# An attention stage with its products with v in one run per head pair, and its sums moved behind the next scores

## The chip, the cores and the metric

The kernel runs on one core of one Trainium2 chip. The metric is the time of one execution on the device in microseconds (us): 1064.72 us is the median of the three runs before (1062.84 to 1065.97). The engines are named as in the profile: PE is TensorE (matrix products and transposes), PEld its weight loads, DVE is VectorE, ACT is ScalarE, POOL is GpSimd, SP is SyncE, which here only issues DMAs. An engine works through its instructions in the order in which they were written into its queue.

## The reference

The kernel computes an attention of 4 batches x 12 heads over 448 positions with head size 64, with soft-capped scores, and two feed-forward layers on its output:

```
scores = q @ k.T / 8;  scores = cap * tanh(scores / cap)
attn   = exp(scores - max) / (sum(exp(scores - max)) + 1e-9)
x      = (attn @ v)  as 1792 x 768
h1     = x @ w_in1;  x1 = (h1 - tanh(h1)) @ w_out1
h2     = x1 @ w_in2; out = (h2 * sigmoid(1.702 * h2)) @ w_out2
```

The weights come as float64, and the kernel converts them on the way. All products are in fp32.

## The kernel before

The first 200 us are attention, the rest the two layers. Only attention is touched by the change, and all of its instructions are pinned: each engine gets them in the order of the code (`pin`). The DMAs on SP are not pinned; the scheduler places them by its own estimate of when they can go.

**Iterations.** Attention has 24 iterations `g`, each one pair of heads. Scores are computed transposed, keys on the partitions, so that their exponentials can be multiplied with v at once. 448 keys make three chunks of 128 and a rest of 64. The rests of two neighbouring iterations (an even one and the odd one behind it) are put together in one tile of 128 partitions, `tl`. An even iteration and the odd one behind it are called a pair of iterations here.

**What one iteration runs, and on what.**
- `scores` (L526): one chunk, two matmuls, one per head, each on 64 of the 128 rows of PE, so that both run beside each other. Chunk 0 of the next iteration is computed in this one.
- `tail_scores` (L536): the rests' scores of two iterations, four small products on quarters of PE.
- `pair_act` (L545, L547): tanh and exp on ACT, two chunks at a time.
- `pair_pv` (L568): one chunk times v, into the PSUM bank `ps_pv` of the iteration, of which there are two.
- `tail_pv` (L577): the rests of both iterations of a pair times v, four small products, into both `ps_pv` banks.
- `key_adds` (L556 to L558): DVE adds the three chunks and the rest, for the softmax's sum.
- `sums_of_two` (L582): PE sums these over the partitions for the pair before, into a PSUM tile `ps_r`; `add_sums` (L605, L90 with `w<-ps_r`) adds that up on DVE.
- `prep` (L505 to L515, L90): transposes of q and k of iteration `g + 3` on PE, copied out of PSUM by DVE.
- `pair_out` (L90 with `xs<-ps_pv`, L592): DVE copies the finished output, and SP stores part of it.
- Beside these run conversions of weights (`conv_*`), reciprocals (`batch_recip`, L610, halves in iterations 7, 8, 13, 14, 19 and 20), the DMA of the reciprocals to DRAM (`wrow`, L615) and back as broadcast rows (`wb`, L621), and the scaling of finished outputs by them (L666, from iteration 10 on).

**What couples the engines.** The PSUM tiles of the transposes (`ps_qk`) and of the sums (`ps_r`) come from one pool of two buffers, `ps_s`, in turn: a new tile waits until DVE has read the one before the last. The order in which they are asked for is sums, q, k in an even iteration and q, k in an odd one. The scores have two buffers of two banks each, read by ACT.

**The order before.** In an even iteration PE runs: scores of chunks 1 and 2, chunk 0 with v, sums of the pair before, the transposes, chunk 0 of the next scores, the small products with v, chunks 1 and 2 with v. In an odd one: scores of chunks 1 and 2, the transposes, chunk 0 with v, chunk 0 of the next scores, the rests' scores, chunks 1 and 2 with v.

Of the kernel before, what the change touches and what calls it, by code (L numbers as in the profile page):

```python
# [40 lines left out]
def attention_moe_moe(ctx, tc, q, k, v, cap, w_in1, w_out1, w_in2, w_out2, out):  # L41
    nc = tc.nc
    B, H, S, D = q.shape
# [516 lines left out]
    def ps_pv(g):  # L560
        if g not in r_t:
            r_t[g] = ps_v.tile([P, 512], F32, tag="v", name="ps_pv")
        return r_t[g]

    def pair_pv(g, c):
        for j in range(2):
            a = slice(j * D, (j + 1) * D)
            pin(nc.tensor.matmul(  # L568
                ps_pv(g)[a, :S], rawv[g][:, j, c, :], tt[g, c][:, j], start=(c == 0 and g % 2 == 0), stop=(c == KC - 1)
            ))  # L570

    def tail_pv(g):
        for n in (g, g + 1):
            r = tail_rows(n)
            for j in range(2):
                a = slice(j * D, (j + 1) * D)
                pin(nc.tensor.matmul(ps_pv(n)[a, :S], vt[n % 4][r, a], tail(g)[r, j], start=(n > g), stop=False))  # L577

    def sums_of_two(g):
        ps = sum_t[g] = ps_s.tile([P, 512], F32, tag="s", name="ps_r")  # L580
# [47 lines left out]
    def attention():  # L628
        wb = {}

        def x_of(g):
            return [n for n, at in enumerate(split_at) if at == g]

        def x_part(n):
            b, i = divmod(n, NP)
            n = S if b == 0 else CUT
            return i, n, slice(b * S, b * S + n)

        load_qk(0, nc.scalar)
        nc.sync.dma_start(out=capr, in_=cap.partition_broadcast(P))  # L640
        nc.vector.tensor_scalar(
            out=cpos.bitcast(U32), in0=capr.bitcast(U32), scalar1=0x7FFFFFFF, scalar2=None, op0=ALU.bitwise_and
        )
        nc.vector.reciprocal(out=tsc, in_=cpos)
        nc.vector.tensor_scalar(out=tsc, in0=tsc, scalar1=QK_SCALE, scalar2=None, op0=ALU.mult)
        load_qk(1)
        load_v(0)
        load_qk(2)
        load_v(1)

        def prep(g):
            prep_q(g)
            prep_k(g)

        prep(0)
        scores(0, 0)
        prep(1)
        tail_scores(0)
        for g in range(NG):
            pair_act(g, (0, KC) if g % 2 == 0 else (0,))  # L660
            if g - 2 in conv_at:
                conv_hi(early[conv_at.index(g - 2)])
            for n in x_of(g):
                i, w, a = x_part(n)
                x = xs[n][:, :w]
                pin(nc.vector.tensor_tensor(out=x, in0=x, in1=wb.pop(n)[:, :w], op=ALU.mult))  # L666
                hi_pool(xh[i][:, a], x)
            scores(g, 1)
            scores(g, 2)
            last_exp = pair_act(g, (1, 2))  # L670
            if g + 1 in conv_at:
                conv_exp(early[conv_at.index(g + 1)])
            load_v(g + 2)
            if g % 2 == 0:
                pair_pv(g, 0)
            if g % 2 == 0 and g > 0:
                sums_of_two(g - 2)
                add_sums(g - 2)
            if g in conv_at:
                conv_low(early[conv_at.index(g)])  # L680
            if g - 1 in conv_at:
                conv_or(early[conv_at.index(g - 1)])
            for n in x_of(g):
                i, w, a = x_part(n)
                lo_pool(xl[i][:, a], xs.pop(n)[:, :w], xh[i][:, a])
            if g - 2 in conv_at:
                conv_lo(early[conv_at.index(g - 2)])
            if g >= NP and g % NP < 3:
                b = g // NP - 1
                if g % NP:  # L690
                    batch_recip(b, g % NP - 1)
            for n in {0: (2,), 1: (3, 4)}.get(g, (g + 3,)):
                prep(n)
            if g % 2:
                pair_pv(g, 0)
            for n in {0: (3, 4)}.get(g, (g + 4,)):
                load_qk(n)
            for n in x_of(g + 1):
                wb[n] = wb_p.tile([P, S], F32, tag="wb", name="wb")
                i, w, a = x_part(n)  # L700
                w_rows(wb[n][:, :w], 0, i, a.start, a.stop)
            if g in (1, 3):
                dbl_dma()
            if g == NG - 1:
                prepare(1)
                hold[0] = True
                for _ in range(12):
                    next(moe_0)
            scores(g + 1, 0)
            if g % 2:  # L710
                tail_scores(g + 1)
            key_adds(g)
            if g % 2 == 0:
                tail_pv(g)
            pair_pv(g, 1)
            pair_pv(g, 2)
            pair_out(g)
        for _ in range(5):
            next(moe_0)
        hold[0] = False  # L720
        sums_of_two(NG - 2)
        add_sums(NG - 2)
        for half in range(2):
            rec = batch_recip(B - 1, half)
        marks.extend((last_exp.ins, rec.ins))
# [617 lines left out]
```

## Time and profile before

| | |
|---|---|
| runs before | 1064.72 us median, 1062.84 to 1065.97 |
| profiled execution | 1063.6 us, of which the span is 1061.8 us |
| mean granted clock of PE | 0.998 |
| PE busy | 1048.6 us, 99% of the span |
| DVE busy | 821.6 us, 77% |
| ACT busy | 692.4 us, 65% |
| POOL busy | 55.5 us, 5% |

The span is the time from the first to the last instruction. The page's slices are 26.5 us long; attention takes the first seven and a half of them. A timeline row gives the start, the duration, the engine, line and operation, what it writes from what, shapes (partitions x elements), how many instructions were merged, and in brackets the time that the engine stood before it and for whom. An fp32 matmul of the code is two instructions in the trace.

### The profile page before, as it was taken

How to read it: one execution, taken by the hardware profiler on the slowest of the kernel's cores; microseconds unless marked ns; L12 is line 12 of the kernel's file. 1: busy time of each engine (PE TensorE's matmuls, PEld its weight loads, DVE VectorE, ACT ScalarE, POOL GpSimd, SP SyncE). 2: the span in 40 equal slices, each digit the busy share in tenths (PEclk: the TensorE clock that was granted, in tenths of full speed). 3: DMA queues.
4: the chain of work that ended last, by engine and by line, in shares of the span. 5: the costliest groups of instructions: out<-in, count | busy, mean ns of one | idle time of the engine just before them, and what ended most of it. 6: DMA issues, size and time to landing. Idle time of an engine off the chain costs nothing.

```text
span 1061.8 us, 15395 instructions
## 1 busy us (share of the span) xinstructions
PE 1048.6 (99%) x5483; PEld 855.9 (81%) x5483; DVE 821.6 (77%) x1097; ACT 692.4 (65%) x958; POOL 55.5 (5%) x56
## 2 busy tenths in 40 slices
PE   9999989999999999999999999999999999999998
PEld 3333323599999998888878888877899999999998
DVE  4689988899996525988999998686799873438973
ACT  6898878788863415656785756655755755657663
POOL 0113242400000000000000000000000000000000
PEclk9999999999999999999999999999999999999999
DMA  6767777775578877887864853799654554444443
GB/s 145 183 187 220 196 189 217 237 249 210 204 228 258 296 239 266 279 297 255 275 226 149 273 188 91 265 319 299 223 171 132 180 163 121 134 126 142 146 135 107
DMA packets 153749, 218.17 MB, mean 205 GB/s; under 512 B 58381, under 2 KB 101705, under 8 KB 153673
## 3 DMA queue, kind: packets, MB, share of 16 engines
q1 hardware_dynamic: 152376, 216.58, 64.6%
q8 instruction: 43, 0.70, 0.3%
q10 hardware_dynamic: 1296, 0.61, 0.2%
q14 instruction: 34, 0.27, 0.1%
HBM read 158.86 MB, written 58.28 MB: 205 GB/s over the span
## 4 chain that ended last, share of the span: by engine, by line
PE 83%; DVE 7%; DMA 6%; issue 2%; ACT 1%; SPq 1%; DVEq 0%; ACTq 0%
PE ps_o L1193 19%; PE ps_h L911 18%; PE ps_h L1091 13%; PE ps_y L951 9%; PE ps_y L1004 9%; PE ps_sc L526 5%; PE ps_pv L568 5%; DMA wd<-in_moe_w_out_dram 1%; DMA wd<-in_moe_w_in_dram 1%; PE ps_r L582 1%; PE ps_tl L536 1%; DMA whole<-s 1%; DVE wl L93 1%; PE ps_pv L577 1%; PE ps_qk L514 1%
## 5 line engine op out<-in xcount | busy, mean ns | idle before, releaser
L81 ACT CAST rh<-gr 128x512 fp32r<-128x512 f32 (+1 forms) x179 | 103.7, 584 | 101.3 <-PE ps_o L1193 65.2
L911 PE MATMUL ps_h<-x,wh 128*128 128x384 f32 (+1 forms) x672 | 152.9, 358 | 0.0
L93 DVE TENSOR_TENSOR rl<-gr,rh 128x512 fp32r<-128x512 f32 (+1 forms) x179 | 113.8, 641 | 26.4 <-ACT rh L81 25.8
L1193 PE MATMUL ps_o<-wh,rl 128*128 128x384 f32 x392 | 130.9, 334 | 0.0
L1193 PE MATMUL ps_o<-wh,rh 128*128 128x384 f32 x392 | 130.9, 334 | 0.0
L1193 PE MATMUL ps_o<-wl,rh 128*128 128x384 f32 x392 | 130.9, 334 | 0.0
L911 PEld LDWEIGHTS ps_h<-x,wh 128*128 128x128 f32 x672 | 121.1, 188 | 12.0 <-issue 0.7
L93 DVE TENSOR_TENSOR wl<-whole,wh 128x768 fp32r<-128x768 f32 (+1 forms) x103 | 93.9, 912 | 14.7 <-ACT wh L81 13.3
L1091 PE MATMUL ps_h<-x,wh 128*128 128x384 f32 (+1 forms) x336 | 97.2, 359 | 0.0
L81 ACT CAST wh<-whole 128x768 fp32r<-128x768 f32 (+1 forms) x103 | 82.4, 800 | 22.7 <-PE ps_h L1091 10.0
L911 PE MATMUL ps_h<-x,wl 128*128 128x384 f32 (+1 forms) x384 | 88.1, 363 | 0.0
L545 ACT ACTIVATE t<-ps_sc,tsc 128x896 f32<-128x896 f32 x72 | 69.8, 1006 | 25.4 <-PE ps_sc L526 24.8
L911 PEld LDWEIGHTS ps_h<-x,wl 128*128 128x128 f32 x384 | 69.8, 188 | 9.7 <-issue 1.4
L1193 PEld LDWEIGHTS ps_o<-wh,rh 128*128 128x128 f32 x392 | 73.6, 188 | 0.0
L1193 PEld LDWEIGHTS ps_o<-wl,rh 128*128 128x128 f32 x392 | 73.6, 188 | 0.0
L1193 PEld LDWEIGHTS ps_o<-wh,rl 128*128 128x128 f32 x392 | 73.6, 188 | 0.0
L547 ACT ACTIVATE t<-t,cpos 128x896 f32<-128x896 f32 x72 | 72.4, 1042 | 0.4
L361 DVE TENSOR_TENSOR gr<-gr 128x512 f32<-128x512 f32 (+2 forms) x112 | 69.2, 645 | 0.8 <-DMA gr<-xa 0.5
L526 PE MATMUL ps_sc<-qk 64*128 64x448 f32 x288 | 68.7, 576 | 0.8 <-ACT qk L81 0.6
L1091 PE MATMUL ps_h<-x,wl 128*128 128x512 f32 (+1 forms) x192 | 69.5, 362 | 0.0
L361 DVE TENSOR_TENSOR part<-ps_h,part 128x512 f32<-128x512 f32 (+1 forms) x48 | 29.8, 621 | 50.8 <-PE ps_h L1091 50.7
L219 DVE SCALAR_TENSOR_TENSOR wr<-wr,wd 128x768 uint32<-128x768 uint32 x48 | 46.6, 972 | 27.5 <-ACT wd L211 21.3
(155 smaller groups left out, 2193.2 us busy)
## 6 DMA issues: line engine op xcount, KB each, us to landing
wd<-in_moe_w_in_dram SPq DMA_DIRECT2D x64, 384.0 KB
wd<-in_moe_w_out_dram SPq DMA_DIRECT2D x29, 768.0 KB
whole<-single SPq DMA_DIRECT2D x36, 384.0 KB
whole<-s SPq DMA_DIRECT2D x33, 384.0 KB
wh<-kept SPq DMA_DIRECT2D x25, 384.0 KB
wl<-kept SPq DMA_DIRECT2D x25, 384.0 KB
single<-wr SPq DMA_DIRECT2D x24, 384.0 KB
whole<-t SPq DMA_DIRECT2D x22, 384.0 KB
```

Source lines behind the costliest of these rows:

```text
L81: pin(nc.scalar.copy(out=dst, in_=src))
L93: return pin(nc.vector.tensor_tensor(out=dst, in0=src, in1=hi.bitcast(F32), op=ALU.subtract))
L361: nc.vector.tensor_tensor(out=out, in0=a, in1=b, op=kind)
L526: pin(nc.tensor.matmul(ps[:, j, :S], qk[a, kc], qk[a, :S], start=True, stop=True))
L545: pin(nc.scalar.activation(out=t, in_=ps[:, :, :S], func=AF.Tanh, scale=tsc))
L547: ins = pin(nc.scalar.activation(out=tt[g, c], in_=tt[g, c], func=AF.Exp, scale=cpos))
L568: pin(nc.tensor.matmul(ps_pv(g)[a, :S], rawv[g][:, j, c, :], tt[g, c][:, j], start=(c == 0 and g % 2 == 0), stop=(c == KC - 1)))
L911: pin(nc.tensor.matmul(ps, w[:, kk, :], x[kk][:, a], start=(m == 0), stop=(m == len(seq) - 1)))
L951: nc.tensor.matmul(bank[e][:, :a1 - a0], w[:, kk, c], x[2 * j + kk][:, a0:a1], start=(j == 0 and m == 0), stop=(j == KF // 2 - 1 and m == ...
L1004: nc.tensor.matmul(ps[e], w[:, kk, c], x, start=(name == head and k == 0 and m == 0), stop=(k == KH - 1 and m == 2), skip_group_check=True,)
L1091: nc.tensor.matmul(ps, w, x, start=(name == head and m == 0), stop=(m == len(seq) - 1), skip_group_check=True,)
L1193: nc.tensor.matmul(ps[n], x[:, t], w[:, kk, :], start=(first and k == 0 and m == 0), stop=(k == KH - 1 and m == 2), skip_group_check=True,)
```

## The change

Five things are written in another place; no function is new.

- Chunk 0 with v is no longer computed early: all three chunks of an iteration stand in one run at its end (in the last iteration chunk 0 stays ahead of the first products of the feed-forward layer).
- The small products with v of a pair move from the even iteration, where they stood behind the next scores, to the odd one, behind the rests' scores of the next pair. The accumulation of an even iteration's bank now begins with its chunk 0 and ends with the small products, hence the new `start` and `stop`.
- The sums of the pair before move from ahead of the transposes to behind the next scores.
- Their addition on DVE (`add_sums`) moves behind `key_adds`.
- `pair_out` of both iterations of a pair is at the end of the odd one.

```diff
@@ pair_pv
-  ps_pv(g)[a, :S], rawv[g][:, j, c, :], tt[g, c][:, j], start=(c == 0 and g % 2 == 0), stop=(c == KC - 1)
+  ps_pv(g)[a, :S], rawv[g][:, j, c, :], tt[g, c][:, j], start=(c == 0 and g % 2 == 0), stop=(c == KC - 1 and g % 2 == 1)
@@ tail_pv
-  pin(nc.tensor.matmul(ps_pv(n)[a, :S], vt[n % 4][r, a], tail(g)[r, j], start=(n > g), stop=False))
+  pin(nc.tensor.matmul(ps_pv(n)[a, :S], vt[n % 4][r, a], tail(g)[r, j], start=(n > g), stop=(n == g)))
@@ attention, in the loop over g
             load_v(g + 2)
-            if g % 2 == 0:
-                pair_pv(g, 0)
-            if g % 2 == 0 and g > 0:
-                sums_of_two(g - 2)
-                add_sums(g - 2)
...
             for n in {0: (2,), 1: (3, 4)}.get(g, (g + 3,)):
                 prep(n)
-            if g % 2:
-                pair_pv(g, 0)
...
             if g == NG - 1:
+                tail_pv(g - 1)
+                pair_pv(g, 0)
                 prepare(1)
...
             scores(g + 1, 0)
             if g % 2:
                 tail_scores(g + 1)
+                if g < NG - 1:
+                    tail_pv(g - 1)
+            elif g:
+                sums_of_two(g - 2)
             key_adds(g)
-            if g % 2 == 0:
-                tail_pv(g)
-            pair_pv(g, 1)
-            pair_pv(g, 2)
-            pair_out(g)
+            if g % 2 == 0 and g:
+                add_sums(g - 2)
+            for c in range(1 if g == NG - 1 else 0, KC):
+                pair_pv(g, c)
+            if g % 2:
+                pair_out(g - 1)
+                pair_out(g)
```

Three places show how the rows move. The first is PE, from the end of iteration 2 to the end of iteration 3, before (one row is one or more matmuls of the code; `x4` is how many):

```order
L577 MATMUL ps_pv<-tl,vt_140 64x448 x2
L577 MATMUL ps_pv<-tl,vt_141 64x448 x2
L568 MATMUL ps_pv<-t,rv 64x448 x4
L526 MATMUL ps_sc<-qk 128x448 x4
L505 MATMUL ps_qk<-ident,raw 128x112 x4
L514 MATMUL ps_qk<-ident,raw 128x128 x3
L515 MATMUL ps_qk<-ident,raw 128x64
L568 MATMUL ps_pv<-t,rv 64x448 x2
L526 MATMUL ps_sc<-qk 128x448 x2
L536 MATMUL ps_tl<-qk 64x448 x4
L568 MATMUL ps_pv<-t,rv 64x448 x4
```

And the same place now:

```order
L582 MATMUL ps_r<-ts,sel 32x448 x4
L568 MATMUL ps_pv<-t,rv 64x448 x6
L526 MATMUL ps_sc<-qk 128x448 x4
L505 MATMUL ps_qk<-ident,raw 128x112 x4
L514 MATMUL ps_qk<-ident,raw 128x128 x3
L515 MATMUL ps_qk<-ident,raw 128x64
L526 MATMUL ps_sc<-qk 128x448 x2
L536 MATMUL ps_tl<-qk 64x448 x4
L577 MATMUL ps_pv<-tl,vt_140 64x448 x2
L577 MATMUL ps_pv<-tl,vt_141 64x448 x2
L568 MATMUL ps_pv<-t,rv 64x448 x6
```

The six products with v stand in one run, the small ones (`vt`) directly behind the rests' scores, the sums directly ahead of the even iteration's run with v, and the scores directly behind the transposes.

The second place is DVE, from the last key addition of iteration 13 through iteration 14, which has a reciprocal, before:

```order
L558 TENSOR_TENSOR ts<-ts,t 128x896
L90 COPY xs<-ps_pv 128x448
L666 TENSOR_TENSOR xs<-xs,wb 128x448
L90 COPY w<-ps_r 128x448
L213 TENSOR_SCALAR wd<-wd 128x768
L610 RECIPROCAL w<-w 128x224
L90 COPY qk<-ps_qk 128x448 x2
L556 TENSOR_TENSOR ts<-t 128x896
L557 TENSOR_TENSOR ts<-ts,tl 64x896
L558 TENSOR_TENSOR ts<-ts,t 128x896
L90 COPY xs<-ps_pv 128x448
```

And now:

```order
L558 TENSOR_TENSOR ts<-ts,t 128x896
L90 COPY xs<-ps_pv 128x448 x2
L666 TENSOR_TENSOR xs<-xs,wb 128x448
L213 TENSOR_SCALAR wd<-wd 128x768
L610 RECIPROCAL w<-w 128x224
L90 COPY qk<-ps_qk 128x448 x2
L556 TENSOR_TENSOR ts<-t 128x896
L557 TENSOR_TENSOR ts<-ts,tl 64x896
L558 TENSOR_TENSOR ts<-ts,t 128x896
L90 COPY w<-ps_r 128x448
```

The copy of the sums has gone behind the key additions, and two output copies stand where one was.

The third place is SP's queue of DMAs around the reciprocals of the second batch, before:

```order
L592 DMA xd_93<-xs 128x448
L465 DMA raw<-in_q_dram 112x4x64 x2
L615 DMA wrow_98<-w 3x320 x4
L615 DMA wrow_99<-w 3x128 x4
L489 DMA rv<-in_v_dram 128x2x192
L621 DMA wb<-wrow_98 64x320
L592 DMA xd_94<-xs 128x448
L621 DMA wb<-wrow_98 64x320
L189 DMA wd<-in_moe_w_in_dram 128x3x256 x2
```

And now:

```order
L592 DMA xd_93<-xs 128x448
L615 DMA wrow_98<-w 3x320 x4
L615 DMA wrow_99<-w 3x128 x4
L621 DMA wb<-wrow_98 64x320 x2
L465 DMA raw<-in_q_dram 112x4x64
L489 DMA rv<-in_v_dram 128x2x192
L465 DMA raw<-in_q_dram 112x4x64
L189 DMA wd<-in_moe_w_in_dram 128x3x256 x2
```

The two broadcast rows stand directly behind the store of the reciprocals, and the two loads of q behind them. On ACT and POOL no row of attention moves, and behind attention no row moves on PE, DVE, ACT or POOL.

## Rows read from the trace of the kernel before

**Rows 1.** The page's busy table: busy time, share of the span, instructions.

```profile
PE 1048.6 (99%) x5483; PEld 855.9 (81%) x5483; DVE 821.6 (77%) x1097; ACT 692.4 (65%) x958; POOL 55.5 (5%) x56
```

**Rows 2.** Stretches: length, busy PE, PEld, DVE, ACT, POOL, clock, DMA, GB/s.

```profile
36.00:52.00 16.00, 15.79 (x92) 5.71 (x90) 11.84 (x15) 13.99 (x15) 3.60 (x2) 1.00 0.60 147
100.00:116.00 16.00, 15.79 (x94) 5.80 (x91) 14.86 (x16) 13.63 (x15) 9.88 (x7) 1.00 0.72 207
120.60:136.20 15.60, 15.39 (x91) 5.52 (x89) 15.04 (x18) 13.96 (x16) 4.68 (x5) 1.00 0.68 200
```

**Rows 3.** Timeline of PE, second half of iteration 12 and iteration 13.

```profile
109.88 1.07 PE L526 MATMUL ps_sc<-qk 64*128 64x448 f32 x4
110.88 0.98 PE L577 MATMUL ps_pv<-tl,vt 64*64 64x448 f32 x8
111.79 1.72 PE L568 MATMUL ps_pv<-t,rv 128*64 128x448 f32 x8
113.44 1.77 PE L526 MATMUL ps_sc<-qk 64*128 64x448 f32 x8
...
116.22 0.97 PE L568 MATMUL ps_pv<-t,rv 128*64 128x448 f32 x4
117.12 1.02 PE L526 MATMUL ps_sc<-qk 64*128 64x448 f32 x4
118.07 0.98 PE L536 MATMUL ps_tl<-qk 64*64 64x448 f32 x8
118.98 1.72 PE L568 MATMUL ps_pv<-t,rv 128*64 128x448 f32 x8
120.64 1.77 PE L526 MATMUL ps_sc<-qk 64*128 64x448 f32 x8
```

**Rows 4.** PE's waits, whole span: us in total, times, longest.

```profile
PE ps_qk L514 <- DVE w L605: 3.9, 6, 2.9
...
PE ps_qk L514 <- DVE w L90: 0.9, 4, 0.2
PE ps_y L1004 <- DVE wl L93: 0.7, 1, 0.7
...
PE ps_qk L514 <- DMA raw<-in_k_dram: 0.5, 1, 0.5
```

**Rows 5.** Who waited for the sums of L582: us, times.

```profile
  DVE w L605: 10.4, 6
  DVE w L90: 5.9, 4
```

**Rows 6.** Timeline of DVE in iteration 14.

```profile
124.27 0.62 DVE L90 COPY w<-ps_r 128x448 f32<-128x448 f32 x1 [0.30 <-PE ps_r L582]
124.81 1.41 DVE L213 TENSOR_SCALAR wd<-wd 128x768 uint32<-128x768 uint16 x1
...
127.61 1.08 DVE L90 COPY qk<-ps_qk 128x448 f32<-128x448 f32 x2
```

**Rows 7.** Timeline of DVE at the start of iteration 16.

```profile
142.67 0.49 DVE L666 TENSOR_TENSOR xs<-xs,wb 128x320 f32<-128x320 f32 x1 [2.78 <-DMA wb<-wrow]
```

**Rows 8.** Timeline of PE in iteration 16.

```profile
143.75 0.55 PE L514 MATMUL ps_qk<-ident,raw 128*128 128x128 f32 x3 [2.86 <-DVE w L605]
...
144.23 1.91 PE L526 MATMUL ps_sc<-qk 64*128 64x448 f32 x4
...
147.78 1.72 PE L568 MATMUL ps_pv<-t,rv 128*64 128x448 f32 x8
```

**Rows 9.** The stretch behind that wait, columns as in rows 2.

```profile
144.00:148.00 4.00, 4.00 (x18) 1.11 (x18) 3.97 (x5) 1.77 (x2) 2.64 (x2) 0.57 0.72 196
```

**Rows 10.** Timeline of SP's DMA issues ahead of that wait.

```profile
130.35 2.27 SPq L465 DMA_DIRECT2D raw<-in_q_dram  x2
132.71 2.65 SPq L615 DMA_DIRECT2D wrow<-w  x8
...
137.07 0.49 SPq L621 DMA_DIRECT2D wb<-wrow  x1
```

## The prediction, made before the changed kernel ran

> **What bounds the kernel now.** The first view to read is the page's busy table: TensorE (PE) is busy for 1048.6 us of the span of 1061.8 [rows 1], so whatever shortens PE's row of work shortens the kernel, and nothing else does. The change lies in the attention stage, which is the first 200 us. The table by stretches shows two regimes there [rows 2]: early, VectorE (DVE) has work for 11.84 us of 16; later, when the finished pairs are scaled as well, for 14.86 of 16 and 15.04 of 15.6. In the second regime DVE is nearly a second bound, and that is what makes the case hard. ScalarE (ACT) has 13.63 to 13.99 in the same stretches and is third.
>
> The timeline of PE shows how its time is made [rows 3]. I read it from start to start, since the ends are modelled. Four instructions of one chunk with v cost 0.90 us when they stand alone (116.22 to 117.12), eight in one run cost 1.65 (111.79 to 113.44), so a further chunk in a run costs 0.75 and a run of its own 0.15 more. The small products of the rests' scores cost 0.91 (118.07 to 118.98), those with v also 0.91 (110.88 to 111.79), each as a run of its own. A chunk of scores costs 0.95 ahead of the rests' scores (117.12 to 118.07) and 1.00 straight behind the transposes (109.88 to 110.88).
>
> The table of PE's waits adds the only wait that repeats [rows 4]: the k transposes wait for the addition of the sums out of PSUM, six times for 3.9 us, the longest 2.9, and four short times for 0.9. Without the longest that is 1.9 us in nine pairs, 0.21 each. The counterpart stands on DVE: it idles 10.4 and 5.9 us, 16.3 in ten even iterations, until the sums are there [rows 5].
>
> **The change part by part.** No matmul is added or removed; three things move.
>
> *Chunk 0 joins chunks 1 and 2.* One run of 12 costs 1.65 + 0.75 = 2.40 in place of 0.90 + 1.65: 0.15 less in each iteration. In odd ones the scores now stand behind the transposes, at 1.00 for 0.95: 0.05 back.
>
> *The small products with v move from the even iteration behind the rests' scores of the odd one.* Both are runs of the same shape, so I cost the second at the step of a further chunk, 0.75 for 0.91: 0.16 less. No row shows these two adjacent; the bounds are 0.91 (no gain) and 0.75. I take 0.75, since every run of one shape in the rows continues at that step.
>
> A chunk of scores costs 0.05 more behind the transposes than behind a run with v, although the last transpose and the scores use PE in one shape (64 rows, 128 columns). The Trainium skill ("TensorEngine Tiling (Array Packing)", Key Properties) says that changing the tiling mode drains TensorE. By it a pair's ten changes of shape in place of fourteen would give 4 x 0.15 and the 0.21 of the wait below, 0.81 for the 0.62 that I work out, 1.9 us more over ten pairs. This row speaks against it, so the sum goes by the rows.
>
> *The sums move from ahead of the transposes to behind the next scores, and their addition on DVE behind the key additions.* The 0.21 wait goes. For a pair in the steady state: even 0.15 + 0.21, odd 0.15 - 0.05 + 0.16, together 0.62. Ten even and nine odd iterations with transposes (2 to 20): 10 x 0.36 + 9 x 0.26 = **5.9 us** off PE's row. The last three iterations have no transposes, and there the scores also merge; I give them 0.5, because ACT is close behind PE there.
>
> *The start.* In iteration 1 PE waits 0.47 us for raw k to land [rows 4]. The small products leave iteration 0, ahead of that transfer, and return behind it. An odd iteration grows by 0.75 - 0.15 + 0.05 = **0.65 us**, and here no shorter even one makes up for it.
>
> *A new wait.* The PSUM buffers of transposes and sums are a ring of two. The order was sums, q, k; it is now q, k, sums. So sums must wait until DVE has copied out this iteration's q, where before they waited for a copy of the iteration before. PE asks for that buffer 2.78 us (scores and transposes, 113.44 to 116.22) plus 1.00 into the even iteration, at 3.78. If it is late, the three chunks with v and the next scores queue behind sums, and ACT after them. Iteration 14, which has a reciprocal, is the worst place [rows 6]: the iteration starts at 120.64 and the q and k copies at 127.61, 6.97 later; two copies take 1.08, so q is out at 7.51. Of this the idle 0.30 before the sums' addition goes, the addition (0.54) is replaced by the second output copy (half of 1.08), and the odd iteration before is 0.65 longer: 6.56, that is 2.8 late. One iteration stands in the rows for four of this pattern: the same working gives 1.8 at iteration 8, 1.0 at 12 and 0.4 at 20, and up to 1 for the k transposes of 13, which need the sums' addition; at the others q is out in time. From the other side the cost is nothing: the 16.3 us that DVE gets back lie in the iterations before these [rows 5], and each stall gives DVE time to catch up. Both ends, 0 and 6.9; the DVE rows of the busy stretch are nearer to the late end, the early ones to the other, and I take **3.2**.
>
> *The event at 140 us.* Once DVE waits 2.78 us for the broadcast row `wb` [rows 7]. It holds the sums' addition, PE's k transposes wait 2.86 behind it [rows 8], and in the next 4 us PE is granted 0.57 of its clock, a stretch partly at 1.2 GHz instead of 2.4 [rows 9]. The scores and the small products then take 3.55 (144.23 to 147.78) for 1.91 (109.88 to 111.79). Price: 2.86 + 1.64 = 4.5 us. The change moves the DMAs: `wb` is issued straight behind `wrow`, without two loads of q ahead (2.27) and without a v load and an output between (135.36 to 137.07 less one `wb`, 1.2) [rows 10]. `wb` would be some 3.5 us earlier, at 139.2, while DVE asked at 142.67 - 2.78 = 139.9 and will ask perhaps 1.5 earlier. A wait of about 0.7 remains, and sums now stand later. Ends: 0 and 4.5 of gain; I take **3.3**, as the order of the issues is nearest to the row of the transfer.
>
> Sum: 0.65 - 5.9 - 0.5 - 3.3 + 3.2 = -5.9 us. Behind attention PE has no wait over 0.7 us [rows 4], and its order there is the same, so the gain passes to the end. The profiled execution took 1063.6 us, 1.8 around the span; 1063.6 - 5.9 = 1057.7. The median of the runs shown is 1.1 above that execution: **1058.8 us**.
>
> **Rivals.**
> *DVE takes it all back.* All stalls come (6.9) and the `wb` wait stays: 0.65 - 5.9 - 0.5 + 6.9 = +1.2, 1065.9. For it speaks 15.04 of 15.6 us [rows 2], against it the idle time handed back.
> *Free of stalls.* DVE is always ahead and the event goes: 0.65 - 5.9 - 0.5 - 4.5 = -10.3, 1054.4. For it speak the 11.84 us of the early regime, against it the reciprocals.
> *Sums stand behind the reciprocal, and the clock falls.* If DVE uses the returned time for nothing (its three additions wait for ACT's exponentials all the same), q is out at 7.51 in iterations 8, 14 and 20, PE stands 3.7 us each time, and a stand of 2.86 already cost 1.64 in clock: 3 x 5.3 = 16.0, with 1.0 at 12. That gives 0.65 - 5.9 - 0.5 - 3.3 + 17.0 = +8.0, 1072.7. It makes the kernel slower once the stalls together pass 9.1 us. Against it speaks that DVE's time is mostly work, not waits, in front of these copies.
>
> **How the numbers follow.** Forecast 0.50, DVE takes it all 0.20, free of stalls 0.18, clock falls 0.12. About 0.3%, 3.2 us, is what a measurement of this kernel can tell. Of the forecast's half, which runs from 1054.5 to 1062.5, nine tenths lie below 1061.5; with the stall-free case and a little of the first rival: faster 0.62. The rest of these is within: 0.26. Slower 0.12. The range reaches from the stall-free case (1054.4, and 0.9 below it for merged runs that may give more) to the first rival (1065.9): 1053.5 to 1066.
>
> **What would show it.** Runs of 12 with v at 2.4 us and the small products at about 1.66 with the rests' scores; no wait of k transposes for the sums' addition in most pairs; instead waits of sums for the q copies, at 8, 12 and 14 first; the clock at 1.00 from 144 to 148. The steady pair 0.6 shorter in the early regime, less in the later. Wrong would be a small step of 0.91 behind the rests' scores, waits of sums in every even iteration, or a granted clock that falls in other places.

## The result, and the profile after

| | before | changed |
|---|---|---|
| median of five runs | 1065.06 us (1062.84 to 1065.97) | 1055.68 us (1054.08 to 1056.18) |
| ratio, with its 95% interval | | 0.9912 [0.9898, 0.9927] |
| profiled execution, span | 1063.6, 1061.8 | 1055.68, 1053.9 |

The kernel is faster by 9.4 us of the medians; 5.9 were forecast (1058.8, range 1053.5 to 1066). The page's busy table answers to [rows 1]:

```profile
PE 1038.7 (99%) x5483; PEld 857.8 (81%) x5483; DVE 819.6 (78%) x1097; ACT 692.0 (66%) x958; POOL 56.1 (5%) x56
```

The number of PE's instructions is the same, its busy time 9.9 us less, the other engines' within 2 us. The same matmuls stand in fewer separate runs, and PE's granted clock is 1.00 throughout.

Three stretches of attention, with the columns of [rows 2]:

```profile
36.00:52.00 16.00, 16.00 (x100) 6.76 (x100) 12.75 (x18) 15.44 (x18) 2.66 (x2) 1.00 0.66 168
100.00:116.00 16.00, 14.09 (x86) 5.42 (x84) 15.69 (x17) 13.86 (x16) 6.53 (x4) 1.00 0.72 191
116.00:132.00 16.00, 15.29 (x94) 5.99 (x92) 15.19 (x20) 13.17 (x15) 5.98 (x5) 1.00 0.65 191
```

Early, PE has no gap at all and ACT is at 15.44 of 16. Around iteration 13 (the second row) PE has gaps of 1.9 us, and DVE is at 15.69: there DVE sets the time, as experiment 8 shows for this place.

An undisturbed pair of iterations on PE, odd (from its transposes) and even, for [rows 3]:

```profile
51.64 0.27 PE L515 MATMUL ps_qk<-ident,raw 64*128 64x64 f32 x1
51.65 1.07 PE L526 MATMUL ps_sc<-qk 64*128 64x448 f32 x4
52.65 0.98 PE L536 MATMUL ps_tl<-qk 64*64 64x448 f32 x8
53.45 0.93 PE L577 MATMUL ps_pv<-tl,vt 64*64 64x448 f32 x8
54.32 2.48 PE L568 MATMUL ps_pv<-t,rv 128*64 128x448 f32 x12
56.72 1.77 PE L526 MATMUL ps_sc<-qk 64*128 64x448 f32 x8
58.43 0.60 PE L505 MATMUL ps_qk<-ident,raw 112*128 112x112 f32 x4
58.87 0.49 PE L514 MATMUL ps_qk<-ident,raw 128*128 128x128 f32 x3
59.29 0.27 PE L515 MATMUL ps_qk<-ident,raw 64*128 64x64 f32 x1
59.30 1.07 PE L526 MATMUL ps_sc<-qk 64*128 64x448 f32 x4
60.30 0.96 PE L582 MATMUL ps_r<-ts,sel 128*32 128x448 f32 x8
61.19 2.48 PE L568 MATMUL ps_pv<-t,rv 128*64 128x448 f32 x12
```

The run of 12 with v takes 2.40 (54.32 to 56.72), rests' scores and small products together 1.67 (52.65 to 54.32). Both are as forecast. The 64-row transpose (L515) and the scores behind it start 0.01 apart; this is what the forecast did not see (below). PE's waits in attention, for [rows 4] (us in total, times, longest):

```profile
PE ps_r L582 <- DVE qk L90: 2.8, 4, 1.2
PE ps_qk L514 <- DVE w L605: 1.8, 2, 1.2
PE ps_sc L526 <- ACT t L545: 1.5, 3, 0.7
```

The k transposes' wait for the sums' addition is gone from all but two iterations; in its place sums wait for the q copies in 8, 12, 14 and 20 (0.23, 0.67, 0.71 and 1.21), the places of the forecast. The two of the second row are at 13 (1.23) and 19 (0.56). The cause of the one at 13 stands on DVE and POOL; here are the three key additions of iteration 12 and the sums' addition on DVE, then, in the same time, POOL's last step on an output and its part of a weight conversion:

```profile
105.30 1.61 DVE L556 TENSOR_TENSOR ts<-t 128x896 f32<-128x896 f32 x1
106.94 1.59 DVE L557 TENSOR_TENSOR ts<-ts,tl 64x896 f32<-64x896 f32 x1
108.64 2.52 DVE L558 TENSOR_TENSOR ts<-ts,t 128x896 f32<-128x896 f32 x1
111.08 0.61 DVE L605 TENSOR_TENSOR w<-w,ps_r 128x448 f32<-128x448 f32 x1
```

```profile
104.81 1.15 POOL L87 TENSOR_TENSOR x<-xs,x 128x448 fp32r<-128x448 f32 x1
105.90 1.69 POOL L84 CAST wh<-wr 128x768 fp32r<-128x768 f32 x1
107.67 2.53 POOL L87 TENSOR_TENSOR wl<-wr,wh 128x768 fp32r<-128x768 f32 x1
```

Of the 72 additions 51 take 1.08 or 1.09. The third here, queued at 108.64, ends 0.96 behind POOL's subtraction, and the first two end 0.95 and 0.94 behind the POOL operations of 104.81 and 105.90. The Trainium skill ("SBUF — State Buffer", "SBUF: two separate sides") says that a DVE operation with two SBUF inputs and a GpSimd operation that reads SBUF exclude each other for whole instructions; the trace agrees, 2.52 for 1.09.

The event at 140 us is gone. SP issues the reciprocals' rows as follows, for [rows 10], and the stretch of [rows 9] now has the full clock:

```profile
126.38 2.50 SPq L615 DMA_DIRECT2D wrow<-w  x8
128.93 1.12 SPq L621 DMA_DIRECT2D wb<-wrow  x2
...
132.17 1.08 SPq L189 DMA_DIRECT2D wd<-in_moe_w_in_dram  x2
```

```profile
144.00:148.00 4.00, 4.00 (x28) 1.34 (x22) 3.86 (x4) 4.00 (x6) 1.74 (x2) 1.00 0.65 205
```

**Where the time went.** I count from the first of an iteration's eight scores instructions to the next iteration's. A normal even iteration went from 8.36 to 6.87, an odd one from 7.20 to 7.65: a pair from 15.56 to 14.52, 1.04 less. Over ten even (-1.49 each) and nine odd iterations (+0.45 each) that is -10.85. The event was 13.23 - 8.36 = 4.87 and is gone. What iterations take above these normal values in the changed kernel, the stalls, is 5.42 (0.31, 0.75, 1.45, 0.78, 0.07, 0.78, 1.28 at 8, 12, 13, 14, 17, 19, 20). The last three iterations give +0.42, the start -0.04, and a start-up that was 0.43 longer in this execution lies ahead of all that. Together -9.5; the first product behind attention starts at 187.84 for 197.32, -9.48.

Behind attention 1.6 of it are lost in the two profiled executions (span -7.9), but not in the medians (-9.4): the profiled execution of before lay 1.5 under its own median.

### The profile page after: what moved, and what is told of

Read it like the earlier page. It is cut to its first block, busy times and chain, and to the rows that moved or that the text cites. A ratio compares the mean times of both kernels' runs of the same rounds, so it can differ in the third digit from the quotient of the medians.

```text
span 1053.9 us, 15397 instructions
## 1 busy us (share of the span) xinstructions
PE 1038.7 (99%) x5483; PEld 857.8 (81%) x5483; DVE 819.6 (78%) x1097; ACT 692.0 (66%) x958; POOL 56.1 (5%) x56
## 4 chain that ended last, share of the span: by engine, by line
PE 81%; DVE 11%; ACT 3%; DMA 3%; issue 2%; SPq 0%; DVEq 0%; ACTq 0%
PE ps_o L1194 19%; PE ps_h L912 19%; PE ps_h L1092 19%; PE ps_y L952 9%; PE ps_y L1005 5%; PE ps_pv L568 3%; PE ps_sc L526 3%; DVE gr L361 1%; DVE wl L93 1%; ACT t L545 1%; DVE rl L93 1%; DVE ts L557 1%; PE ps_r L582 1%; DVE ts L556 1%; PE ps_tl L536 1%
```

## The experiments

Iteration times below are read from starts of scores in each profile. "2 to 7" is from the start of iteration 2 to that of 8, "8 to 19" from there to the start of 20; "16" is that iteration. The ratio is to runs of the kernel before on the same chip; those had medians of 1064.52 (experiments 1 to 4), 1064.21 (5 to 8), 1065.51 (9 to 11) and 1063.76 (12).

| kernel | 2 to 7 | 8 to 19 | 16 | median us | ratio [95%] |
|---|---|---|---|---|---|
| before | 46.68 | 98.21 | 13.23 | | |
| changed | 43.56 | 91.25 | 6.87 | 1055.68 | 0.9912 [0.9898, 0.9927] |
| 1 run with v merged | 45.33 | 99.31 | 16.20 | 1063.28 | 0.9992 [0.9977, 1.0006] |
| 2 small products moved | 46.19 | 96.32 | 8.51 | 1068.08 | 1.0032 [1.0014, 1.0050] |
| 3 sums moved | 45.38 | 91.77 | 7.94 | 1057.95 | 0.9941 [0.9924, 0.9958] |
| 4 rows issued earlier | 46.68 | 96.87 | 8.99 | 1063.99 | 0.9994 [0.9977, 1.0012] |
| 5 64-row transpose first | 45.32 | 92.38 | 7.17 | 1058.39 | 0.9941 [0.9927, 0.9955] |
| 6 reciprocals late | 43.56 | 96.84 | 14.18 | 1060.30 | 0.9963 [0.9949, 0.9977] |
| 7 sums last | 43.56 | 92.01 | 7.15 | 1056.98 | 0.9926 [0.9913, 0.9940] |
| 8 conversions late | 43.56 | 94.81 | 6.87 | 1074.02 | 1.0084 [1.0066, 1.0101] |
| 9 four reciprocals late | 43.56 | 93.90 | 6.87 | 1057.63 | 0.9929 [0.9913, 0.9945] |
| 10 last step late | 43.56 | 94.14 | 7.35 | 1066.03 | 1.0011 [0.9998, 1.0024] |
| 11 = 9 and 10 | 43.56 | 94.53 | 7.36 | 1067.13 | 1.0014 [1.0001, 1.0028] |
| 12 merged, sums moved | 44.04 | 92.80 | 8.53 | 1058.88 | 0.9952 [0.9934, 0.9970] |

### One part of the change at a time (from the kernel before)

**1. The run with v merged, nothing else.**

```diff
-            if g % 2 == 0:
-                pair_pv(g, 0)
...
-            if g % 2:
+            if g == NG - 1:
                 pair_pv(g, 0)
...
-            pair_pv(g, 1)
-            pair_pv(g, 2)
+            for c in range(1 if g == NG - 1 else 0, KC):
+                pair_pv(g, c)
```

(`start` and `stop` follow the new order here and in experiment 2; those lines are left out.)

> The kernel before, with chunk 0 with v joined to chunks 1 and 2 in one run in every iteration; the sums, their addition and the small products stay where they stood. Theory (every change of the shape in which PE is used costs 0.15 to 0.20 us, from transposes to scores too): 0.15 less in the even and 0.30 to 0.35 less in the odd iterations, about 0.45 to 0.5 per pair, 4.5 to 5 us over ten pairs, so about 1060 against 1065; the scores behind the transposes of an odd iteration start 0.87 after the last transposes' run began. The wait of the k transposes for the sums' addition stays, and so does the event at iteration 16. Rival (the prediction's reading: scores behind transposes cost 0.05 more than scores behind a run with v, nothing is saved there): 0.15 and 0.10, 0.25 per pair, 2.5 us, about 1062.5. Second rival (DVE bounds the stage): nothing at all, DVE's waits shrink by as much.

Even iterations 8.22, odd 6.90: 0.15 and 0.30 less, as the theory has it, against the prediction's 0.15 and 0.10. The median is only 1.2 us lower, which the interval does not tell from nothing: the iterations before and behind are shorter, but the event grew to 16.20 - 8.22 = 8.0 us. The even iteration in this kernel still has the sums ahead of the transposes:

```profile
60.16 0.60 PE L505 MATMUL ps_qk<-ident,raw 112*128 112x112 f32 x4
60.97 0.55 PE L514 MATMUL ps_qk<-ident,raw 128*128 128x128 f32 x3 [0.21 <-DVE w L605]
61.45 0.27 PE L515 MATMUL ps_qk<-ident,raw 64*128 64x64 f32 x1
61.46 1.07 PE L526 MATMUL ps_sc<-qk 64*128 64x448 f32 x4
```

From the q transposes to the scores 1.30, where the changed kernel has 0.87 (58.43 to 59.30): 0.43, of which the trace calls only 0.21 a wait. The rest is in the steps around it: q's run lasts 0.81 for 0.44, which is 0.16 more than the wait, and k's 0.48 for 0.42.

**2. The small products moved, nothing else.**

```diff
             if g % 2:
                 tail_scores(g + 1)
+                tail_pv(g - 1)
             key_adds(g)
-            if g % 2 == 0:
-                tail_pv(g)
...
-            pair_out(g)
+            if g % 2:
+                pair_out(g - 1)
+                pair_out(g)
```

> The kernel before, with the small products with v of a pair moved behind the rests' scores of the odd iteration, and both outputs copied at its end; chunk 0 with v and the sums stay. Theory: the two small runs of one shape side by side save one change of shape, 0.15 to 0.2 per pair (an odd iteration longer by about 0.75, an even one shorter by 0.91 and by the change to chunks 1 and 2), 1.5 to 2 us over ten pairs, about 1063.3. Rival (prediction: 0.16 per pair off, 0.65 lost at the start): about 1064. If the event at iteration 16 goes with it (it hangs on the order of SP), another 4.9 less: then about 1058.5.

Undisturbed iterations take 7.45 and 7.94, a pair 15.39, 0.17 less: the term of 0.16 was right. But the median is 3.6 us worse, which no theory had. Chunk 0 with v stands early in this kernel, and it now meets ACT:

```profile
PE ps_pv L568 <- ACT t L545: 6.2, 6, 2.1
```

The longest of these waits, 2.08 in iteration 22, is followed by a granted clock of 0.57 from 190 to 194, and that iteration takes 9.84 for 8.05. The profiled execution (1065.0) lies 3.1 under its median, so this trace does not show all of the loss.

**3. The sums moved, nothing else.**

```diff
-            if g % 2 == 0 and g > 0:
-                sums_of_two(g - 2)
-                add_sums(g - 2)
...
             if g % 2:
                 tail_scores(g + 1)
+            elif g:
+                sums_of_two(g - 2)
             key_adds(g)
+            if g % 2 == 0 and g:
+                add_sums(g - 2)
```

> The kernel before, with only the sums moved behind the next scores and their addition on DVE behind the key additions. Theory: the k transposes no longer stand behind the sums' addition, which in the timelines cost 0.43 in each even iteration (1.30 from the q run to the k run before, 0.87 after); 0.43 x 10 = 4.3 us less, minus the new waits of sums for the q copies, about 2 to 3 us: about 1063. The wait of 2.86 of iteration 16 moves off the transposes but stays on DVE if the broadcast row is as late. Rival (the prediction's 0.21 per pair out of the table of waits): 2.1 minus 2 to 3, so no change, 1065. The trace tells the two apart without the stalls: the even iteration without a stall is 7.9 by the theory, 8.15 by the rival, from 8.36.

Even iterations 7.94: 0.43 less, the theory's number. The stalls that both theories deducted hardly came (0.79 at 13 and 0.21 at 14, 0.06 at 20), and the event is gone too, its broadcast row being issued at 127.33. This one edit gives 6.6 of the 9.4 us; the event alone is 4.9 in the trace.

The three parts add up where nothing else interferes: in iterations 2 to 7 they take 1.35, 0.49 and 1.30 off 46.68, which makes 43.54; the changed kernel has 43.56. From 8 on they don't: the two that lie on top of the sums would bring another 0.61 per pair, 3.7 in six pairs, and the stretch falls only from 91.77 to 91.25.

**4. The rows of the reciprocals issued earlier; PE, DVE, ACT and POOL as before.**

```diff
+                    with tc.high_priority(offset=120):
                         nc.sync.dma_start(out=wrow[p][n, :, a:z], in_=...)
...
+                if p == 0:
+                    first_of_all.enter_context(tc.high_priority(offset=120))
                 nc.sync.dma_start(out=t[j * D:(j + 1) * D], in_=wrow[p]...)
```

> The kernel before, with the rows of work on PE, DVE, ACT and POOL unchanged; only the DMAs of the reciprocals to DRAM and back are issued earlier on SP. Theory: the event at iteration 16 is the order of SP's queue and nothing else; with the broadcast rows in time it is gone whole, 4.9 us (the iteration takes 8.36 for 13.23): about 1060. Rival (prediction's figure): 3.3 less and a wait of 0.7 left, about 1061.8. Second rival: the transfer is late for the loads it shares the DMA engines with; then nothing, 1065, and DVE still waits more than 2 us for it.

The event is gone (8.99, of which 0.27 a wait for the addition), and DVE waits 0.19 for the row. Yet the median is not clearly lower: three transfers of raw k are now late, and PE waits 0.63 and 1.08 in 17 and 0.86 in 19 for them (17 takes 9.17 and 19 takes 8.12 for 7.20). The place in SP's queue is what the row won and what k lost. The first expectation was right on the event and wrong on the time, since it left out who would lose the place. What decided whether the row was late shows when SP's orders are put side by side: the row's second transfer was issued at 137.07 before (2.78 of wait), 136.07 with the run merged, and in this kernel at 136.75. Before (both halves of the row), with the run merged, then in this kernel:

```profile
135.90 0.50 SPq L621 DMA_DIRECT2D wb<-wrow  x1
...
137.07 0.49 SPq L621 DMA_DIRECT2D wb<-wrow  x1
137.67 1.07 SPq L189 DMA_DIRECT2D wd<-in_moe_w_in_dram  x2
```

```profile
136.07 0.49 SPq L621 DMA_DIRECT2D wb<-wrow  x1
136.67 1.06 SPq L189 DMA_DIRECT2D wd<-in_moe_w_in_dram  x2
```

```profile
136.75 1.77 SPq L625 DMA_DIRECT2D wb<-wrow  x3
138.57 0.58 SPq L592 DMA_DIRECT2D xd<-xs  x1
139.25 1.05 SPq L189 DMA_DIRECT2D wd<-in_moe_w_in_dram  x2
```

And what DVE waited for the row with the run merged:

```profile
141.48 0.49 DVE L666 TENSOR_TENSOR xs<-xs,wb 128x320 f32<-128x320 f32 x1 [5.34 <-DMA wb<-wrow]
```

With a weight load (`wd`) issued 0.6 us behind it, the row arrived 5.4 us after its issue; with the load 2.5 us behind, 2.9. The kernel before has the load 0.60 behind (137.67) and 5.6 to arrival, experiment 6 has it 1.1 ahead and 4.4. These four traces agree, but no run changed the place of the load alone, so this stays a reading. The changed kernel adds nothing to it: its load is 2.7 behind the second half (129.45), but the row is issued 7 us earlier and would be in time either way.

### The price of a change of shape

**5. The 64-row transpose ahead of the three 128-row ones** (from the changed kernel, as all that follow but the last).

```diff
+        pin(nc.tensor.transpose(ps[:, KC * P:S], t[:KT, 1, KC * P:], ident[:KT, :KT]))
...
-        pin(nc.tensor.transpose(ps[:, KC * P:S], t[:KT, 1, KC * P:], ident[:KT, :KT]))
```

> The changed kernel with the 64-row transpose of k ahead of the three 128-row ones, so that a 128-row run stands directly ahead of the scores: the same matmuls, two more changes of shape in each of the 21 iterations with transposes. Theory (a change of shape costs 0.15 to 0.20 us, and scores behind the 64-row transpose pay none): iterations 2 to 7 take 0.3 to 0.4 more each; from 8 on part of it is hidden, since there the stretch from 8 to 20 is set by DVE (91.25 us with the changed kernel, 91.77 with the sums moved alone, though its PE row is 0.6 per pair longer). Sum +3 to +6 us. Rival (the prediction's reading, no price from transposes to scores): no change in iterations 2 to 7 and in the median.

Every iteration from 2 to 7 takes 0.29 or 0.30 more, 1.76 in six: two changes of shape at 0.15 on average. The rival is out.

```profile
52.59 0.27 PE L513 MATMUL ps_qk<-ident,raw 64*128 64x64 f32 x1
52.80 0.55 PE L515 MATMUL ps_qk<-ident,raw 128*128 128x128 f32 x3
53.27 1.02 PE L526 MATMUL ps_sc<-qk 64*128 64x448 f32 x4
```

The small transpose now holds the row for 0.21 instead of 0.01. From 8 to 19 the same twelve additions should cost 3.5, and the stretch grew by 1.1. PE's time is covered there. The median is 2.7 above the changed kernel's, just under the range given; by the ratios it is 3.1.

### What makes the stalls

**6. All reciprocals behind the copies of q and k.**

```diff
+            for n in {0: (2,), 1: (3, 4)}.get(g, (g + 3,)):
+                prep(n)
             if g >= NP and g % NP < 3:
                 b = g // NP - 1
                 if g % NP:
                     batch_recip(b, g % NP - 1)
-            for n in {0: (2,), 1: (3, 4)}.get(g, (g + 3,)):
-                prep(n)
```

> The changed kernel with each half of a reciprocal (1.55 us on DVE, iterations 7, 8, 13, 14, 19, 20) behind the q and k copies of its iteration and not ahead of them. Theory A (the stalls are a matter of order on DVE, a copy behind a reciprocal): the copies are out 1.5 us earlier, the stalls of iterations 8, 13, 14 and 20 (0.31, 1.45, 0.78, 1.28) go: -2.5 to -3.8. Theory B (from iteration 8 on DVE's work sets the time, 85.5 of 91.25 us busy and the rest waits for ACT): the reciprocal then delays the key additions, the sums and the next copies, and the stalls come elsewhere: 0 to -1. A wait of the broadcast rows for the later reciprocal is possible (+0 to +4).

The stalls of 8, 14, 19 and 20 go (6.87, 6.87, 7.65, 6.87), those of 12 and 13 stay. For the four theory A is right: the copies stood behind a reciprocal. But the row of the reciprocals then goes out at 130.23 for 126.38, next to a weight load, DVE waits 5.2 for it, PE stands 5.3 behind that, the clock is at 0.50 from 140 to 144, and iteration 16 takes 7.3 more; I had put that at 4 at most.

**7. The sums at the end of the even iteration.**

```diff
-            elif g:
-                sums_of_two(g - 2)
             key_adds(g)
-            if g % 2 == 0 and g:
-                add_sums(g - 2)
...
+            if g % 2 == 0 and g:
+                sums_of_two(g - 2)
+                add_sums(g - 2)
             if g % 2:
                 pair_out(g - 1)
```

> The changed kernel with the sums and their addition at the end of the even iteration, behind the run with v (2.4 us later on PE, and behind the next iteration's scores on the ring's account). Theory A: sums no longer wait for the q copy (0.67, 0.71, 0.56 and the like at 8, 12, 14, 20: -2 to -2.5), but the transposes of the odd iteration wait for their addition out of the same PSUM ring, 2.8 us behind the sums on PE, DVE having the two output copies of the pair before it no more: together -1 to -2. Theory B (DVE's work sets the time): the stalls only change their place, from sums to transposes, 0 to -0.5 in sum, and the stretch from 8 to 20 stays at about 91 us.

Sums no longer wait, and the transposes of 13 wait longer. The stretch is 92.01, theory B's. (The 0.56 in the expectation was no wait of sums: it is that of the transposes of 19.) Iteration 13 takes 11.36, 3.7 more than normal, and the wait alone (1.97, for 1.23 in the changed kernel) does not explain it; the granted clock behind it does, since 0.38 of 4 us is another 1.5:

```profile
112.00:116.00 4.00, 4.00 (x24) 1.41 (x23) 3.96 (x5) 2.29 (x4) 0.00 (x0) 0.62 0.83 247
```

That is the prediction's third rival, in small. The profiled execution, 1059.33, is the slowest of the six.

**8. The weight conversions beside attention placed later.**

```diff
-    conv_at = [3, 5, 7, 9, 11, 14, 16, 18, 20]
+    conv_at = [3, 5, 7, 9, 15, 17, 18, 20, 21]
```

> The changed kernel with another table of where the weight conversions beside attention stand: 3, 5, 7, 9, 15, 17, 18, 20, 21 for 3, 5, 7, 9, 11, 14, 16, 18, 20. The same work, but DVE has 0.56 + 0.95 less in iterations 11 and 12 and POOL nothing in 13, where the three key additions took 1.61, 1.59 and 2.52 beside POOL's conversions and take 1.09 each without. Theory B (DVE's time sets iterations 12 to 15, 30.9 busy of 32.0 us): the stalls of 13 and 14 go and most of that of 12, 2 to 2.8 us; the conversions added at 15 to 20 lengthen those iterations by up to 1.5; sum -1 to -2.5, and iterations 12 to 15 take 29.5 to 30 for 32.0. Theory A (order on DVE alone): the q copies stay behind additions and reciprocal, stalls of 0.7 stay at 12 and 14, only the 1.2 at 13 shrinks: -0.5 to -1.

Iterations 12 to 15 take 29.04, four normal ones, for 32.02: no stall left, PE without a gap, DVE at 27.56 for 30.89. The columns are those of the stretches above; under it the three additions of iteration 12, one of which still takes 1.71 beside POOL:

```profile
101.41:130.45 29.04, 29.04 (x178) 11.39 (x176) 27.56 (x35) 27.07 (x30) 5.36 (x6) 1.00 0.64 166
```

```profile
105.35 1.71 DVE L556 TENSOR_TENSOR ts<-t 128x896 f32<-128x896 f32 x1
107.09 1.08 DVE L557 TENSOR_TENSOR ts<-ts,tl 64x896 f32<-64x896 f32 x1
108.28 1.09 DVE L558 TENSOR_TENSOR ts<-ts,t 128x896 f32<-128x896 f32 x1
```

Theory B holds for these iterations, reciprocals included, which were not moved here. As a whole it is the worst of all: what was moved stands in the way later (17 takes 11.19 and 19 takes 10.47; PE waits 8.4 us for ACT, for 1.5 in the changed kernel), and the first product behind attention waits 9.6 for a converted weight. I had counted 1.5 for that.

**9. The reciprocals behind the copies only in 7, 8, 19 and 20.**

```diff
+                if g % NP and b == 1:
                     batch_recip(b, g % NP - 1)
...
+            if g >= NP and g % NP in (1, 2) and g // NP != 2:
+                batch_recip(g // NP - 1, g % NP - 1)
```

> The changed kernel with the reciprocal behind the q and k copies in iterations 7, 8, 19 and 20 only; in 13 and 14 it stays ahead, so that the row of the reciprocals goes to DRAM as early as in the changed kernel. Theory (the run with all reciprocals late lost by the broadcast row alone, 7.3 us at iteration 16, and won the stalls of 8, 19 and 20): iteration 16 takes 6.87, 19 and 20 take 7.65 and 6.87 for 8.43 and 8.15; -2 us against the changed kernel, about 1053.5. Rival (the reciprocals' work only moves, DVE's time sets the stretch): iterations 17 to 22 give it back, 0.

Iteration 16 and 20 are as expected (6.87), 8 too. But rows now come late again: DVE waits 5.2 us for them in five places, first 1.35 at iteration 10, and 10, 12 and 17 to 19 take 0.6 to 1.4 more than normal. The gain is given back as the rival has it, but by way of the rows; what part DVE's work has in it stays open.

**10. The last step of a conversion on DVE behind the additions.**

```diff
-            if g - 1 in conv_at:
-                conv_or(early[conv_at.index(g - 1)])
...
             if g % 2 == 0 and g:
                 add_sums(g - 2)
+            if g - 1 in conv_at:
+                conv_or(early[conv_at.index(g - 1)])
```

> The changed kernel with the last step of a weight conversion on DVE (0.95 us, every second even iteration up to 12, then 15, 17, 19, 21) behind the key additions and the sums' addition instead of ahead of the q copy. POOL's part of the conversion is released by it and starts some 5 us later, beside the reciprocal and the copies and not beside the three key additions. Theory (the stall of 1.45 at iteration 13 and those of 0.7 at 12 come from DVE being held by this step and by POOL's part beside its additions): the q copy of 12 is out 0.95 earlier, the additions of 12 take 1.1 to 1.3 each for 1.61, 1.59 and 2.52; stalls of 12 and 13 gone, -2 us, about 1053.5 to 1054. Rival (the additions are slow whatever POOL does, or DVE's work sets the time): the additions still take more than 1.5 each, and no more than 0.75 is gained.

The additions of 12 take 1.81, 1.08 and 1.09, with POOL's part at 111.37, and 13 is normal (7.65): with experiment 8 this shows the conversion as the cause of the stall of 1.45. Its step on DVE and POOL's part moved together, and no run parts them. Iteration 12 keeps its stall (7.76, sums wait 0.82), and 14 takes 8.40 for 7.65: from 12 to 14 only 0.56 is gained (23.81 for 24.37). The stall moved on: at 14 sums wait 1.46 for the q copy, for 0.71 in the changed kernel. Later, conversions on ACT wait 5.4 for their loads, PE waits 5.8 for ACT, and the first product behind attention 4.7 for a weight.

**11. Both edits.** 

> Both of these edits together. Theory: the stalls at 8, 12, 13, 19 and 20 go, about 4 us off the stretch from 8 to 20 (87.5 for 91.25, the pairs then at 14.52 throughout), about 1051 to 1052. Rival (DVE's work sets the stretch): not below 90 for the stretch, and the sum no better than the better of the two alone.

1067.13, 8 to 19 in 94.53: the theory of separate stalls falls. Of the five iterations aimed at, only 8 and 13 become normal (6.87 and 7.65); 12, 19 and 20 take 8.54, 9.83 and 7.91, and the kernel is slower.

**12. The run merged and the sums moved, the small products where they were.**

> The kernel before with chunk 0 with v joined to chunks 1 and 2 and with the sums moved behind the next scores: the changed kernel without the move of the small products. Theory (the parts add up while PE sets the time, and from iteration 8 on DVE's work sets it): even iterations 8.36 - 0.15 - 0.43 = 7.78, odd 6.90, a pair 14.68 for the 14.52 of the changed kernel in iterations 2 to 7; from 8 to 20 between 91 and 92 as with the two others that moved the sums, stalls included; so within 1 us of the changed kernel's 1055.7 if the broadcast row is in time. Rival (the small products' move alone cost 3.6 us beside before, and does so here): 1052, the stretch from 8 to 20 below 90. Second rival (it gives its 0.17 per pair everywhere): 1057.4.

7.79 and 6.89, as the theory has it. But 8 to 19 take 92.80, and it is 1058.88, 3 us above the changed kernel; the second rival is nearest. Sums wait 0.30, 0.84 and 1.12 for the q copy at 8, 12 and 14, and at 16, 18 and 20 PE waits 0.53 each for ACT, which the changed kernel does not do there. PE's waits for ACT in attention:

```profile
PE ps_sc L526 <- ACT t L545: 3.9, 6, 1.3
```

So the small products' move, a loss of 3.6 alone, is worth about 3 beside the other two (4 by the ratios). Its place decides what ACT has ready when; how, no run here isolates.

No version beat the changed kernel by its median; experiment 7 is the nearest, 1056.98, and its interval and that of experiment 9 overlap the changed kernel's.

## Why the prediction was right, and where not

| step | forecast | measured |
|---|---|---|
| pairs, iterations 2 to 20 | -5.9 | -10.85 |
| the last three | -0.5 | +0.42 |
| the event | -3.3 | -4.87 |
| new stalls | +3.2 | +5.42 |
| the start | +0.65 | -0.04 |
| sum | -5.9 | -9.9, and 0.43 of start-up ahead of it |

The direction and the mechanism were right, and the time lies in the range; the largest term was half its size. That the forecast missed by only 3.1 us is in part luck: pairs, event and start came out 7.2 lower than forecast, stalls and the last three 3.1 higher.

- *"A chunk of scores costs 0.05 more behind the transposes."* This step failed. I compared the step of the scores, 1.00 and 0.95, and left out that of the transpose ahead of them, though the trace of before had it: 0.01 ahead of scores of the same 64 rows (they start at 109.88), 0.21 ahead of a run with v (116.22). Odd iterations lose 0.30 by the merge and not 0.10 (experiment 1), and two added changes of shape cost 0.29 per iteration (experiment 5). The rule that I weighed and set aside, in "TensorEngine Tiling (Array Packing)" of the Trainium skill (Key Properties), was the better reading: four changes of shape less are 0.15 + 0.30 + 0.17 = 0.62 in a pair; with the 0.43 of the next point that makes 1.05, and 1.04 was measured.

```profile
109.87 0.27 PE L515 MATMUL ps_qk<-ident,raw 64*128 64x64 f32 x1
116.01 0.27 PE L515 MATMUL ps_qk<-ident,raw 64*128 64x64 f32 x1
```

- *"The 0.21 wait goes."* Right, and mis-sized: it cost 0.43 (experiment 3), since the steps around this wait are longer too (experiment 1). The column of waits was a lower bound here.
- *The small products, 0.16.* Right (0.17, experiment 2).
- *The start, 0.65.* Did not come, and by luck: the wait for raw k of [rows 4] is not among PE's waits after, but these loads are issued as before (the last at 19.86 for 19.82), and PE comes to them 0.44 later by the longer start-up of this execution. Experiment 6, whose code is the same there, waits 0.38 for them, and its iteration 1 takes 9.54 for 9.12.
- *The last three, -0.5.* PE waits 0.35 and 0.51 for ACT at 21 and 22; I named ACT and still counted a gain.
- *The event, 3.3 of 4.5.* It went whole, and was 4.87. The row was issued 7 us earlier (128.93 for 135.90), not 3.5, and no wait of 0.7 stayed.
- *The new wait, 3.2 between 0 and 6.9.* The places were right (8, 12, 13, 14, 20) but for 19, which has 0.78 and was not named; the sizes were not: 8 took 0.31 for 1.8 and 14 took 0.78 for 2.8, 13 took 1.45 and 20 took 1.28 for up to 1 and 0.4. At 14 DVE had got ahead: the q and k copies start 3.74 into the iteration (121.04), for 6.97 before. At 13 POOL's conversion lay on all three key additions, where before it lengthened one, to 2.58 (experiments 8 and 10).
- *The first rival, DVE takes it back.* True of a part: of 3.7 us that merged runs and small products would bring from 8 to 19 beside the sums, 0.5 arrived. *Free of stalls* was right on the event only. *The clock falls* did not come: the changed kernel's stand of 1.23 at 13 left the clock at 1.00, where one of 1.97 at the same place was followed by 0.62 (experiment 7).
- Two small sums of the forecast do not come out, and neither moves it: the new waits as listed make 7.0 and not 6.9, and the parts of "faster" make 0.63 ahead of the first rival's share, not 0.62.

## What to carry to other kernels

Cost a change of order on PE by the start-to-start time of everything from one run ahead of the moved instructions to one behind: the price of a change of shape, and part of the price of a wait, lies in the neighbours' steps and not in the column of waits. Then ask at every place what the next engine has left: the same 0.61 us per pair was worth all of itself where DVE had 3 us to spare in 16, and nearly nothing where it had none. And look at each small transfer's neighbours in the issue queue, since an edit that moves no DMA in the code (experiment 3) had this row issued 8.6 us earlier.

## What the runs showed of the hardware that was not expected

- A change of the shape in which PE is used costs 0.15 us on average in these fp32 runs (experiment 5: 1.76 us for twelve), also between a transpose and scores; a 64-row transpose and 64-row scores behind it start 0.01 apart.
- A wait of 0.21 on PE cost 0.43 (experiment 3).
- Three DVE additions with two SBUF inputs, each queued beside a POOL operation, ended 0.94 to 0.96 behind it, up to 2.52 us for 1.09 (changed kernel, iteration 12).
- What PE's stands did to the granted clock: 1.23 us left it at 1.00; 1.97 was followed by 0.62 over 4 us (experiment 7), 2.08 by 0.57 (experiment 2), 5.4 by 0.50 (experiment 1, 144 to 148), the level of 1.2 GHz for the whole stretch. The length of a stand does not decide it alone: in experiment 8 one of 3.47, ended at 148.51, left the clock at 1.00, and one of 2.75, ended at 166.88, was followed by 0.65:

```profile
148.00:152.00 4.00, 2.99 (x16) 1.43 (x16) 1.56 (x3) 4.00 (x6) 3.87 (x3) 1.00 0.67 223
168.00:172.00 4.00, 4.00 (x18) 1.96 (x16) 1.24 (x2) 4.00 (x5) 0.00 (x0) 0.65 1.01 371
```

- The second half of a broadcast row (64 x 320 numbers) took 4.4 to 5.6 us from its issue to its arrival with a weight load issued within 1.1 us of it, and 2.9 with the load 2.5 us behind (four traces; no run moved the load alone).
